# Float64 weights made float32 by a product on ScalarE instead of a clamp

## The chip, the core and the metric

The kernel runs on one core of one Trainium2 chip. The core has a matrix engine (TensorE; PE in the profile, and PEld for its weight loads), VectorE (DVE), ScalarE (ACT), GpSimd (POOL) and SyncE (SP), which here issues the loads. Each engine works through its own queue of instructions in order, and engines wait for each other by semaphores. The metric is the time of one execution on the device, in microseconds.

## What is computed

Three stages follow each other. Attention over 4 batches of 8 heads with 1152 positions of width 64, whose queries are pooled in pairs to 576; a mixing of the positions with two thin matrices and a two-layer network; and a gated unit with a normalisation and a product over positions:

```python
q_pool = q.reshape(B, H, S // 2, 2, D).mean(axis=3)
attn = softmax(scale * q_pool @ k.T) @ v           # 4 x 8 x 576 x 64
x = attn laid out as B x 576 x 512
u = x + ((x.T @ U) @ V).T                          # U 576 x 32, V 32 x 576
x = u + relu(u @ w_ch1) @ w_ch2                    # 512 x 2048, 2048 x 512
h = relu(x @ w_in); u, v = halves of h             # 512 x 1024
v_s = w_spatial @ normalised(v) + b_spatial
out = (u * v_s) @ w_out                            # 512 x 512
```

U, V, w_ch1, w_ch2, w_in and w_out are drawn as float32 and multiplied by a float64 number, so that they reach the kernel as float64. The core reads such a weight as two words of 32 bits, a low and a high one, and has to make a float32 of them.

## The kernel before

**Stages.** The attention is cut into units of 128 pooled queries (one head, or two halves of two heads); a unit is a set of score matmuls over 1152 keys, a row maximum, an exponential and the product with the values. The first five pairs of heads (units 0 to 44) take an extra step for the row's maximum ("peak"): a small product whose result, a row of 1x128, ScalarE copies out of PSUM into the tile of the queries' low part, and the next score matmuls read that tile. Beside the units of the attention the mixing and the network of each batch run as soon as its heads are there, and behind them comes the gated unit.

**Weights.** The weights are converted while the attention runs. Generators prepare w_ch2 and w_ch1 in two halves h (`w2_prep`, `w1_prep`); they are advanced between unit 13 and unit 39 for h = 0 and between unit 39 and unit 59 for h = 1. `low_rank_weights` converts U and V at the start. `w_in_split` and `w_split` convert w_in and w_out much later, at 748 to 896 us of the profiled execution. The first half of w_ch1 comes in four chunks of 128x1024 values, each loaded by SyncE into a buffer (tiles 113, 114 and 115 of the group ml), converted into tile 110, squared back into its buffer for a norm, and split into two 16-bit halves scaled by that norm. The buffers of the first half are three and are used in turn, also by w_ch2, so the load of a chunk has to wait until ScalarE has written the last square into its buffer. The first and the fourth chunk of w_ch1 use tile 113.

**The conversion.** `conv64_part` makes float32 from the words in five steps: Abs of the high word on ScalarE, taken as a float32; a clamp of that value between two constants; a shift by three with a mask on VectorE; the sign and top bit from the high word, by a mask and an or; and the low word's upper bits, by a shift and an or. The clamp holds the exponent where the shift can't overflow. It is 36 times an instruction of GpSimd (for U, V, w_ch1 and w_ch2) and 24 times one of VectorE (for w_in and w_out).

**What sets the order.** The kernel's functions issue nothing by themselves. A recorder takes each operation with what it reads and writes, gives it a cost by engine and size (`charge`, lines 174 to 210; a clamp on GpSimd counts 250 ns and 0.85 ns for each column and holds a port that VectorE's larger operations need as well), and a list scheduler puts all of them in an order, forwards by a priority and backwards by the latest start, eight times over, and takes the order that ends first (`issue`, lines 293 to 316). It does so three times in the program. Every instruction is issued from line 316, so the profile shows line 316 for all of them, and operations are told apart by engine and tile: `at` is attention, `ml` weights and the network, `co` small statistics, `ma` the gated unit, `xa` its weights, `ps` PSUM.

## Time and profile before

| | us |
|---|---|
| median of three runs | 1043.31 |
| lowest and highest run | 1041.41, 1043.6 |
| span of the profiled execution | 1043.4 |
| TensorE busy in it | 983.6 |
| VectorE busy | 778.7 |
| ScalarE busy | 631.8 |
| GpSimd busy | 310.6 |

The profiled execution is one run of the program, seen by the profiler; its span goes from the first to the last instruction. Its time stands 0.1 over the median. A number in brackets at the end of a row of the timeline is the idle time of the engine just before that row, and the arrow names what ended it. The granted clock is TensorE's; 1.00 is 2.4 GHz and 0.50 is 1.2 GHz.

### The profile page before, as it was taken

Reading aid. Unit: us, or ns where it says so; the run is one execution under the profiler, and the core shown is the slowest. Engines: PE = TensorE matmul, PEld = TensorE weight load, DVE = VectorE, ACT = ScalarE, POOL = GpSimd, SP = SyncE. Lnnn points to the kernel's source line nnn. Section 1 sums busy time; section 2 is a strip of 40 time slices with the busy share of each in tenths; the row PEclk is TensorE's granted clock in tenths of the full one; section 3 lists DMA queues with packets and bytes.
Section 4 is the critical chain, followed back from the end, with each engine's and each line's share of the span. In section 5 each row is a group of like instructions: output and inputs, shape, how many; then the busy total and the mean of one; then the engine's idle time right before and its main releaser. Section 6 shows DMA issues by size and latency. Waiting matters only on the chain.

```text
span 1043.4 us, 26123 instructions
## 1 busy us (share of the span) xinstructions
PE 983.6 (94%) x10797; PEld 790.5 (76%) x10797; DVE 778.7 (75%) x1645; ACT 631.8 (61%) x1170; POOL 310.6 (30%) x342
## 2 busy tenths in 40 slices
PE   4888889989899999999999999999899999999998
PEld 3677778768777778778887878888677857784787
DVE  5796879899998889888788998755693289646540
ACT  6776797877785667667666766654471147344322
POOL 1544445155442433345342533331000005002100
PEclk9998999999999999999999999999999999999999
DMA  9964446289988979899796988676460062220002
GB/s 240 241 166 107 115 109 153 73 190 210 175 162 140 195 130 198 157 156 183 137 200 102 192 165 124 117 136 116 159 203 1 30 213 86 68 71 29 3 1 92
DMA packets 270616, 139.34 MB, mean 134 GB/s; under 512 B 249152, under 2 KB 254016, under 8 KB 269472
## 3 DMA queue, kind: packets, MB, share of 16 engines
q1 hardware_dynamic: 270496, 137.67, 61.8%
q8 instruction: 84, 1.38, 0.5%
q14 instruction: 36, 0.29, 0.1%
HBM read 69.29 MB, written 9.44 MB: 75 GB/s over the span
## 4 chain that ended last, share of the span: by engine, by line
PE 63%; DVE 15%; DMA 8%; ACT 7%; issue 4%; POOL 2%; SPq 1%; ACTq 0%; DVEq 0%; POOLq 0%
PE ps L316 63%; DVE co L316 7%; ACT at L316 4%; DVE at L316 3%; DVE ml L316 3%; DMA ml<-in_w_dram 3%; DMA at<-at 3%; ACT ml L316 3%; POOL at L316 1%; SPq L316 1%; DMA at<-in_kT_dram 1%; DVE xa L316 1%; DVE ma L316 1%; DMA at<-in_qT_dram 1%; DMA at<-in_v_dram 1%
## 5 line engine op out<-in xcount | busy, mean ns | idle before, releaser
L316 PE MATMUL ps<-ml,ml 128*128 128x288 f16 x3072 | 410.5, 287 | 9.6 <-DVE ml L316 5.1
L316 PEld LDWEIGHTS <-ml 128*128 128x128 f16 x3072 | 290.6, 98 | 95.3 <-issue 24.2
L316 PE MATMUL ps<-at,at 128*64 128x65 f32 (+6 forms) x2892 | 246.3, 279 | 24.9 <-ACT at L316 24.4
L316 PEld LDWEIGHTS ps<-at,at 128*64 128x64 f32 (+2 forms) x2892 | 197.4, 162 | 54.0 <-ACT at L316 34.9
L316 DVE TENSOR_REDUCE co<-ps 128x1 f32<-128x1152 f32 (+1 forms) x166 | 200.6, 1210 | 48.2 <-PE ps L316 33.7
L316 ACT ACTIVATE at<-ps,co 128x1152 f32<-128x1152 f32 x99 | 120.7, 1219 | 64.4 <-DVE co L316 60.3
L316 POOL TENSOR_TENSOR at<-at 128x1152 f16<-128x1152 f32 (+1 forms) x54 | 114.8, 2127 | 62.0 <-ACT at L316 29.9
L316 ACT ACTIVATE ml<-ps 128x288 f16<-128x288 f32 x128 | 51.8, 406 | 89.1 <-PE ps L316 89.0
L316 PE MATMUL ps<-ma,ma 128*128 128x288 f16 (+2 forms) x676 | 105.2, 318 | 0.0
L316 POOL TENSOR_SCALAR co<-co,co 128x1 f32<-128x1 f32 x99 | 39.7, 401 | 217.9 <-ACT at L316 206.1
L316 PEld LDWEIGHTS <-at 128*128 128x128 f16 (+1 forms) x2970 | 90.6, 101 | 13.6 <-issue 7.4
L316 ACT CAST at<-at 128x1152 f16<-128x1152 f32 (+3 forms) x90 | 93.1, 1044 | 11.0 <-PE ps L316 5.5
L316 PE MATMUL ps<-at 128*128 128x64 f16 (+1 forms) x2970 | 95.3, 194 | 3.2 <-DVE co L316 2.2
L316 PE MATMUL ps<-xa,xa 128*128 128x288 f16 (+1 forms) x600 | 94.8, 320 | 1.3 <-ACT ma L316 1.3
L316 PEld LDWEIGHTS <-xa 128*128 128x128 f16 x600 | 58.5, 98 | 36.7 <-issue 2.0
L316 POOL TENSOR_TENSOR at<-at,at 128x1152 f16<-128x1152 f32 (+2 forms) x30 | 68.7, 2290 | 43.9 <-ACT at L316 41.7
L316 DVE SCALAR_TENSOR_TENSOR ml<-ps,ml 128x288 f16<-128x288 f32 x128 | 57.6, 451 | 31.1 <-ACT ml L316 30.5
L316 ACT ACTIVATE at<-at 128x1152 f16<-128x1152 f32 (+1 forms) x61 | 65.7, 1076 | 13.5 <-PE ps L316 9.4
L316 ACT ACTIVATE at<-ps 128x512 f32<-128x512 f32 (+2 forms) x100 | 57.7, 602 | 19.7 <-PE ps L316 18.9
L316 DVE SCALAR_TENSOR_TENSOR ml<-ml,co,ml 128x288 f16<-128x288 f32 (+1 forms) x85 | 63.4, 771 | 3.4 <-ACT ml L316 3.4
L316 ACT ACTIVATE ml<-ml,co 128x288 f16<-128x288 f32 (+2 forms) x96 | 52.1, 592 | 10.8 <-DVE co L316 9.7
L316 ACT CAST ma<-ma 128x288 fp32r<-128x288 f32 (+1 forms) x50 | 24.8, 498 | 53.6 <-DVE ma L316 53.5
(85 smaller groups left out, 1114.8 us busy)
## 6 DMA issues: line engine op xcount, KB each, us to landing
at<-in_qT_dram SPq DMA_DIRECT2D x42, 288.0 KB, 5.0
at<-in_kT_dram SPq DMA_DIRECT2D x42, 288.0 KB, 4.8
xa<-x2d SPq DMA_DIRECT2D x16, 576.0 KB, 4.9
ml<-in_w_dram SPq DMA_DIRECT2D x8, 1024.0 KB, 6.1
at<-in_v_dram SPq DMA_DIRECT2D x11, 576.0 KB, 4.9
ml<-in_w_dram SPq DMA_DIRECT2D x8, 512.0 KB, 6.7
at<-in_w_dram SPq DMA_DIRECT2D x8, 512.0 KB, 4.3
xa<-in_w_in_dram SPq DMA_DIRECT2D x8, 512.0 KB, 4.9
```

The lines of the kernel that those rows point to most:

```text
L316: getattr(eng, method)(*args, **kwargs)
```

## The change

The clamp goes. ScalarE multiplies the high word, taken as a float32, with 2 to the -112, which moves the exponent to its place and makes a number that is too small a zero; the shift's mask then keeps the whole exponent, and the sign alone comes from the high word. The two switches that chose the clamp's engine go as well.

```diff
-CL = 0
-CL1 = 0
...
-TOPBITS = -0x40000000
-F64MIN = 2.0 ** -15 * 1.125
-F64MAX = 122879.9921875
+SIGNBIT = -0x80000000
+F64SC = 2.0 ** -112
...
-    def conv64_part(F, raw, clamp):
+            conv64_part(F[:, i * n:(i + 1) * n], raw[:, i * n:(i + 1) * n, :])
+
+    def conv64_part(F, raw):
         lo, hi = raw[:, :, 0], raw[:, :, 1]
         Fi = F.bitcast(I32)
-        act.activation(F, hi.bitcast(F32), AF.Abs)
-        clamp = clamp or (dve if CL else pool)
-        clamp.tensor_scalar(F, F, F64MAX, F64MIN, op0=ALU.min, op1=ALU.max)
-        dve.tensor_scalar(Fi, Fi, 3, 0x3FFFFFF8, op0=ALU.logical_shift_left, op1=ALU.bitwise_and)
-        dve.scalar_tensor_tensor(Fi, hi, TOPBITS, Fi, op0=ALU.bitwise_and, op1=ALU.bitwise_or)
+        act.activation(F, hi.bitcast(F32), AF.Copy, scale=F64SC)
+        dve.tensor_scalar(Fi, Fi, 3, 0x7FFFFFF8, op0=ALU.logical_shift_left, op1=ALU.bitwise_and)
+        dve.scalar_tensor_tensor(Fi, hi, SIGNBIT, Fi, op0=ALU.bitwise_and, op1=ALU.bitwise_or)
         dve.scalar_tensor_tensor(Fi, lo, 29, Fi, op0=ALU.logical_shift_right, op1=ALU.bitwise_or)
...
-                conv64_part(Fs[i + k], words(a, DM), dve if CL else pool)
+                conv64_part(Fs[i + k], words(a, DM))
...
-            conv64(F, words(t, n), dve if CL1 else pool)
+            conv64(F, words(t, n))
...
-        conv64(F, words(t, n), dve)
+        conv64(F, words(t, n))
...
-            conv64(Fs[i], words(t, DM), dve)
+            conv64(Fs[i], words(t, DM))
```

The instruction counts of the two programs differ by 36 on GpSimd (tensor-scalar operations, 135 before and 99 after) and by 24 on VectorE (483 and 459). Each program has two loads of ScalarE's function tables. The scheduler solves the order anew: the matmuls stand in another order up to the one with the number 6698 of 9790 and alike from there on, which is at about 745 us of the profiled execution. The instructions now carry line 313.

The first place is ScalarE's queue at the first chunk of w_ch1 (first half). `ml_113,co_131` is the Square out of the chunk's buffer for an earlier part of w_ch2, `ml_110<-ml_113` the chunk's conversion; `at_104<-ps_70` are exponentials, `at_100` and `at_101` the tiles that the peaks are copied to. Before, from the first row behind the last Square `ml_113,co_131`:

```order
L316 ACTIVATE at_104<-ps_70 128x320
L316 CAST at_98<-at_97 128x576
L316 CAST at_93<-at_92 128x1152
L316 ACTIVATE at_104<-ps_70 128x512
L316 CAST at_100<-at_97 64x576
L316 ACTIVATE ml_115,co_142<-ml_110 128x512
L316 ACTIVATE at_104<-ps_70 128x512
L316 CAST at_101<-ps_70 1x128
L316 ACTIVATE ml_115,co_142<-ml_110 128x512
L316 ACTIVATE at_104<-ps_70 128x256
L316 ACTIVATE at_104<-ps_70 128x512 x2
L316 ACTIVATE ml_110<-ml_113 128x512 x2
```

After, from the fourth row behind the last Square `ml_113,co_131`:

```order
L313 ACTIVATE at_104<-ps_70 128x640
L313 ACTIVATE ml_115,co_142<-ml_110 128x512
L313 ACTIVATE at_104<-ps_70 128x640 x2
L313 CAST at_101<-ps_70 1x128
L313 ACTIVATE ml_108<-ml_110,co_150 128x512
L313 ACTIVATE at_104<-ps_70 128x640
L313 CAST at_98<-at_97 128x576
L313 CAST at_93<-at_92 128x1152
L313 CAST at_101<-ps_70 1x128
L313 ACTIVATE at_104<-ps_70 128x320
L313 CAST at_100<-at_97 64x576
L313 ACTIVATE ml_110<-ml_113 128x512
```

Before, the last Square out of the buffer has eleven rows between it and the conversion; after, it stands four rows ahead of this piece, with fourteen rows between it and the first conversion, and the chunk's two halves are converted apart from each other.

The second place is ScalarE's queue at the fourth chunk, which uses the same buffer. `ml_113,co_141` are the Squares of the first chunk, `ml_110<-ml_113` again the conversion. Before, from the second Square:

```order
L316 ACTIVATE ml_113,co_141<-ml_110 128x512
L316 CAST at_100<-ps_70 1x128
L316 ACTIVATE ml_110<-ml_110,co_149 128x512
L316 ACTIVATE ml_108<-ml_110,co_149 128x512
L316 CAST ml_108<-ml_110 128x512
L316 ACTIVATE at_104<-ps_70 128x512
L316 ACTIVATE at_104<-ps_70 128x256
L316 ACTIVATE at_104<-ps_70 128x512
L316 CAST at_100<-ps_70 1x128
L316 ACTIVATE at_104<-ps_70 128x512
L316 ACTIVATE ml_110<-ml_114 128x512 x2
L316 CAST at_100<-ps_70 1x64
```

After, from the two Squares:

```order
L313 ACTIVATE ml_113,co_141<-ml_110 128x512 x2
L313 ACTIVATE at_104<-ps_70 128x320
L313 CAST at_99<-at_97 128x576
L313 CAST at_94<-at_91 128x1152
L313 CAST at_100<-ps_70 1x128
L313 CAST at_101<-at_97 64x576
L313 ACTIVATE ml_110<-ml_110,co_149 128x512
L313 ACTIVATE ml_108<-ml_110,co_149 128x512
L313 CAST ml_108<-ml_110 128x512
L313 ACTIVATE ml_110<-ml_113 128x512
L313 ACTIVATE ml_110<-ml_114 128x512
L313 CAST at_100<-ps_70 1x128
```

Before, the conversion of the fourth chunk comes as the second row behind this piece, behind another small cast, thirteen instructions after the second Square. After, it is the tenth row of the piece, eight instructions after the second Square, and the third chunk's conversion (`ml_110<-ml_114`) and a peaks' copy come behind it.

## Rows read from the trace of the kernel before

**Rows 1.** The page's busy time, share of the span and instructions of each engine.
```profile
PE 983.6 (94%) x10797; PEld 790.5 (76%) x10797; DVE 778.7 (75%) x1645; ACT 631.8 (61%) x1170; POOL 310.6 (30%) x342
```

**Rows 2.** Windows by stage: length, engines' busy us, granted clock, DMA share, GB/s.
```profile
14.00:330.00 316.00, 281.96 (x3643) 239.55 (x3643) 270.38 (x490) 236.91 (x464) 138.23 (x144) 0.98 0.71 160
330.00:740.00 410.00, 403.20 (x5096) 329.06 (x5093) 325.76 (x620) 260.05 (x429) 144.45 (x165) 1.00 0.83 150
...
748.00:839.00 91.00, 91.00 (x745) 72.70 (x744) 54.68 (x171) 39.81 (x91) 0.00 (x0) 1.00 0.24 81
839.00:876.00 37.00, 35.43 (x206) 19.94 (x205) 31.95 (x94) 22.75 (x49) 10.45 (x9) 1.00 0.63 199
```

**Rows 3.** Waits of TensorE, 0 to 330 us: total us, times, longest.
```profile
PE ps L316 <- ACT at L316: 24.5, 19, 9.8
PE ps L316 <- DVE co L316: 14.9, 15, 1.9
```

**Rows 4.** Timeline around the longest wait: start, us, instruction, idle before and its releaser.
```profile
85.70 1.21 ACT L316 ACTIVATE ml<-ml 128x512 f32<-128x512 f32 x2 [3.66 <-DMA ml<-in_w_dram]
...
86.94 0.26 ACT L316 CAST at<-ps 1x128 fp32r<-1x128 f32 x1
...
87.24 4.83 PE L316 MATMUL ps<-at,at 128*128 128x384 f32 x45 [4.40 <-ACT at L316]
```

**Rows 5.** Chain of waits, 70 to 112 us: issue, us to landing, transfer.
```profile
75.42 10.20 DMA ml<-in_w_dram
...
100.84 8.07 DMA ml<-in_w_dram
```

**Rows 6.** Windows around the longest wait and around one at 43.67 us.
```profile
40.00:60.00 20.00, 17.64 (x251) 15.03 (x250) 15.55 (x19) 16.88 (x34) 12.56 (x13) 1.00 0.73 201
...
87.20:91.80 4.60, 4.56 (x43) 4.23 (x45) 3.60 (x5) 2.74 (x4) 1.85 (x2) 0.50 0.02 8
```

**Rows 7.** Timeline of TensorE at 43.67 us.
```profile
43.67 1.64 PE L316 MATMUL ps<-at,at 128*128 128x384 f32 x37 [1.62 <-ACT at L316]
```

**Rows 8.** Groups by line and form, ScalarE: busy us, mean ns, idle before.
```profile
L316 ACT ACTIVATE at<-at 128x1152 f16<-128x1152 f32 x50 | 58.1, 1163 | 2.0 <-DMA at<-at 1.2
L316 ACT CAST at<-at 128x1152 f16<-128x1152 f32 x49 | 56.4, 1151 | 0.7
```

**Rows 9.** Groups by line and form, weights (ml) and late weights (xa).
```profile
L316 POOL TENSOR_SCALAR ml<-ml 128x512 f32<-128x512 f32 x32 | 22.7, 714 | 40.5 <-ACT ml L316 39.9
...
L316 DVE TENSOR_SCALAR ml<-ml 128x512 int32<-128x512 int32 x32 | 17.5, 563 | 5.9 <-POOL ml L316 5.9
...
L316 DVE TENSOR_SCALAR xa<-xa 128x256 f32<-128x256 f32 x24 | 6.3, 282 | 0.0
```

**Rows 10.** Waits of VectorE, whole span: total us, times, longest.
```profile
DVE ml L316 <- POOL ml L316: 7.3, 6, 3.9
```

**Rows 11.** Timeline of GpSimd and VectorE behind the longest wait.
```profile
86.44 1.19 POOL L316 TENSOR_SCALAR ml<-ml 128x512 f32<-128x512 f32 x2 [5.47 <-ACT ml L316]
...
87.09 0.82 DVE L316 TENSOR_SCALAR ml<-ml 128x512 int32<-128x512 int32 x1 [3.86 <-POOL ml L316]
```

**Rows 12.** Timeline of ScalarE, 69 to 79 us.
```profile
69.52 0.43 ACT L316 COPY ml<-ps 128x320 f32<-128x320 f32 x1
...
77.86 0.66 ACT L316 CAST at<-at 64x576 fp32r<-64x576 f32 x1
```

**Rows 13.** The page's DMA issues: KB each, median us to landing.
```profile
ml<-in_w_dram SPq DMA_DIRECT2D x8, 1024.0 KB, 6.1
```

**Rows 14.** Timeline of ScalarE, 96 to 110 us.
```profile
96.47 2.29 ACT L316 CAST at<-at 128x576 fp32r<-128x576 f32 x3
...
101.28 1.34 ACT L316 ACTIVATE ml<-ml,co 128x512 f32<-128x512 f32 x2 [1.14 <-DVE co L316]
...
108.94 1.23 ACT L316 ACTIVATE ml<-ml 128x512 f32<-128x512 f32 x2 [1.11 <-DMA ml<-in_w_dram]
```

**Rows 15.** View of the weight tiles: shortest, median, longest ns; first, last us.
```profile
L316 DVE TENSOR_SCALAR ml<-ml x36: 202/422/1853, 22.3 to 262.5; 128x512 int32<-128x512 int32 x32, 128x80 int32<-128x80 int32 x2, 96x288 int32<-96x288 int32 x2
```

More of the change, by code (lines that the diff above doesn't have):

```diff
@@ L498, in words, with conv64 @@
         return t[:, :2 * n].bitcast(I32).rearrange("p (n w) -> p n w", w=2)
-    def conv64(F, raw, clamp=None):
+    def conv64(F, raw):
         n = F.shape[1] // SPL
         for i in range(SPL):
-            conv64_part(F[:, i * n:(i + 1) * n], raw[:, i * n:(i + 1) * n, :], clamp)
-    def conv64_part(F, raw, clamp):
+            conv64_part(F[:, i * n:(i + 1) * n], raw[:, i * n:(i + 1) * n, :])
+    def conv64_part(F, raw):
         lo, hi = raw[:, :, 0], raw[:, :, 1]
         Fi = F.bitcast(I32)
-        act.activation(F, hi.bitcast(F32), AF.Abs)
-        clamp = clamp or (dve if CL else pool)
-        clamp.tensor_scalar(F, F, F64MAX, F64MIN, op0=ALU.min, op1=ALU.max)
-        dve.tensor_scalar(Fi, Fi, 3, 0x3FFFFFF8, op0=ALU.logical_shift_left, op1=ALU.bitwise_and)
-        dve.scalar_tensor_tensor(Fi, hi, TOPBITS, Fi, op0=ALU.bitwise_and, op1=ALU.bitwise_or)
+        act.activation(F, hi.bitcast(F32), AF.Copy, scale=F64SC)
+        dve.tensor_scalar(Fi, Fi, 3, 0x7FFFFFF8, op0=ALU.logical_shift_left, op1=ALU.bitwise_and)
+        dve.scalar_tensor_tensor(Fi, hi, SIGNBIT, Fi, op0=ALU.bitwise_and, op1=ALU.bitwise_or)
         dve.scalar_tensor_tensor(Fi, lo, 29, Fi, op0=ALU.logical_shift_right, op1=ALU.bitwise_or)
```

## The prediction

> **What bounds the kernel now.** I read first the engines' shares, then the busy time by stage, then TensorE's waits, and last the instructions around its longest wait. The shares say that TensorE is the engine to look at: it is busy for 983.6 of 1043.4 us, every other engine for at most 778.7 [rows 1]. So the whole program has about 60 us in which TensorE does nothing, and a change that leaves the matmuls alone can win or lose only there, or by moving the granted clock.
>
> The windows by stage say where these 60 us lie [rows 2]. From 14 to 330 us, the stretch in which the weights U, V, w1 and w2 are converted beside the first attention pairs, TensorE is idle for 316.00 - 281.96 = 34.0 us. From 330 to 740 it is idle for 6.8 us of 410. From 748 to 839, where w_in is converted, it is busy for 91.00 of 91.00 us. From 839 to 876, where most of w_out is converted, 1.6 us are left. So what happens on ScalarE, VectorE or GpSimd before 330 us can matter, what happens from 748 to 839 is covered, and a delay or a gain before 330 us is neither absorbed nor doubled later: with 6.8 us of idle time in the next 410 us there is almost no slack in which to hide it.
>
> Inside the first 330 us TensorE waits mostly for ScalarE's attention tiles, 24.5 us in 19 waits (the longest of 9.8 us is the start of the program), and for VectorE's small statistics, 14.9 us in 15 waits [rows 3]. One of these waits touches the conversion. At 87.24 us TensorE has been idle for 4.40 us and is released by ScalarE. ScalarE's own row explains it: at 85.70 it starts the Abs of the first chunk of w1 after 3.66 us of waiting for the transfer of that chunk, and the copy of the peaks, 0.26 us of work that the score matmuls need, stands behind it and starts at 86.94 [rows 4]. The transfer was issued at 75.42, when ScalarE had finished the last Square out of that buffer, and took 10.20 us [rows 5]. The stall has a second price: in the 4.60 us behind it the granted clock is 0.50, that is 1.2 instead of 2.4 GHz, with TensorE busy for 4.56 us [rows 6]. At the full clock this is 2.28 us of work, so 2.28 us are lost. The stall costs 4.40 + 2.28 = 6.7 us in all. A wait need not drop the clock: the one of 1.62 us at 43.67 lies in a window whose clock is 1.00 [rows 6, 7].
>
> **The change part by part.** The sum is made against the profiled execution, whose span is 1043.4 us, 0.1 over the median of 1043.31 us. Four edits are in the diff, and a fifth effect comes from the list scheduler, which solves the order anew once the clamps are gone.
>
> *The operation on ScalarE.* Abs of the high word becomes a copy with a constant scale, the same shape, the same count of 60 (36 for the early weights, 24 for w_in and w_out). The trace has a scaled copy and a plain one of the same shape 128x1152, 1163 and 1151 ns [rows 8]. The constant scale thus costs about 12 ns, 60 x 12 ns = 0.7 us if all of it lay on the path, with nothing as the lower end. I take 0.
>
> *The clamps of w_in and w_out, on VectorE.* 24 instructions of 282 ns are 6.8 us by the mean and 6.3 us by the group's busy time, which counts overlap once [rows 9]. Those of w_in lie where TensorE is busy all the time, and what covers them is the last w1/w2 block's matmuls. Only from 839 to 876 can they show, where TensorE is idle for 1.6 us [rows 2]. Bounds: 0 to -1.6 us; I take -0.5, because most of that idle time belongs to one wait for the gated unit's tiles, not for weights.
>
> *The clamps of the early weights, on GpSimd.* The 32 large ones take 714 ns each, 22.7 us [rows 9], and four small ones add little. GpSimd is busy for 310.6 of 1043.4 us [rows 1] and is no bound; what the clamp costs is a step in the chain ScalarE, GpSimd, VectorE. VectorE waits for GpSimd's weight tiles 7.3 us in 6 waits, the longest 3.9 us [rows 10]. That longest one is the stall above seen from VectorE, which starts the shift at 87.09 [rows 11], so it is counted already. 7.3 - 3.9 = 3.4 us is the most that VectorE gets back; TensorE waits for VectorE only at times, so I take -1.0, between 0 and -3.4.
>
> *The new order at the first chunk of w1.* In the order after, the two Squares out of the buffer stand early, and between the second of them and the conversion there are 15 ScalarE instructions, among them five exponentials and three long casts. In the trace of before nearly the same rows run from the copy at 69.52 to the end of the cast at 77.86, which is 78.52: 9.0 us [rows 12]. After has one Square less and one scaled copy and two tiny casts more, so I estimate 9 us again. The transfer is issued at the start of this stretch instead of its end. It needs 6.1 us (the median of these eight transfers, [rows 13]) to 10.20 us [rows 5]. The head of line then waits 0 to 1.2 us; I take 1.0, nearer to the slow row because it is the same transfer, and no loss of clock, as at 43.67. Gain: 1.0 - 6.7 = -5.7 us, bounds -6.7 and -5.5.
>
> *The new order at the fourth chunk of w1.* It uses the same buffer, and here the order goes the other way. Before, the transfer was issued at 100.84, took 8.07 us, and ScalarE waited 1.11 us for it at 108.94 [rows 5, 14]; thirteen instructions lay in between. After, both Squares stand together and only eight instructions follow before the conversion. Their durations: an exponential of 320 columns, 0.43 (a copy of this size, [rows 12]); the casts of 576, 1152 and 576 columns, 2.29 together [rows 14]; the peaks' copy, 0.26 [rows 4]; two scaled halves, 1.34 [rows 14]; one cast of 512, half of 1.21 = 0.60 [rows 4]. The sum is 4.9 us. With a transfer of 6.1 to 8.07 us ScalarE waits 1.2 to 3.2 us instead of 1.11, and the peaks' copy that TensorE needs stands two rows behind. I take 2.1, net +1.0 us. Bounds: -1.1, if a wait of ScalarE for VectorE in that stretch covers it, and +6.4, if the transfer is as slow as the first chunk's and the clock falls (the slower rival, below).
>
> *The rest of the new order.* Apart from the stall TensorE has 34.0 - 4.4 = 29.6 us of idle time before 330 us, made of some forty short waits. They will be dealt out anew, and the trace of before doesn't show the outcome. Bounds: -2, two waits of about a microsecond less (14.9/15, [rows 3]), and +6, a new stall nearly as dear as the one that goes. I take +2, the middle: the end of one wait lets the next one show.
>
> The sum: 0 - 0.5 - 1.0 - 5.7 + 1.0 + 2.0 = -4.2 us, 1043.4 - 4.2 = **1039 us**.
>
> A rule on the port that VectorE and GpSimd share asks for a larger gain. The row first: at 86.44 GpSimd runs two clamps, 1.19 us long, until 87.63. VectorE starts a shift at 87.09 that takes 0.82 us and ends at 87.91, though the median of the 36 shifts is 0.42; the longest took 1.85 and the 32 large ones have a mean of 563 ns [rows 9, 11, 15]. The Trainium skill, "SBUF — State Buffer", section "SBUF: two separate sides", states that this port pair is an exclusive lock, so that a VectorE operation in its two-port mode and a GpSimd operation block each other for a whole instruction. The row agrees in direction. By that rule 36 GpSimd operations fewer would also shorten VectorE's own instructions, and the sum would be that of the first rival; the forecast leaves them as they are.
>
> **The rivals.**
>
> *The lock goes as well.* VectorE's shifts fall from their mean to their median: 32 x (563 - 422) ns = 4.5 us [rows 9, 15]; GpSimd's step of the chain is worth its whole bound of 3.4; the first and fourth chunks and w_out count as in the forecast, -5.7 + 1.0 - 0.5; and the rest of the order costs nothing. The sum is -13.1 us, 1030 us. For it: VectorE is busy for 270.38 of 316 us before 330 us [rows 2] and TensorE waits for it. Against it: a shorter instruction of VectorE shows only in those of its waits that TensorE shares, 14.9 us in all [rows 3], and the removed clamps may be followed by GpSimd's other work in the same place.
>
> *The gain is given back.* The stall at 87 us goes, but TensorE meets other waits before 330 us for as much: the rest of the order costs its upper bound of 6 instead of 2. Sum -0.2, 1043.2 us: no change that can be measured. For it: 29.6 us of short waits show that ScalarE and VectorE run just abreast of TensorE there, and ScalarE's in-order queue has the same rows as before. Against it: the stall is by far the longest wait after the start.
>
> *The fourth chunk's transfer becomes the stall (slower).* If that transfer takes 10.20 us, as the first chunk's did, ScalarE waits 10.20 - 4.9 = 5.3 us in front of a peaks' copy. At 87 us a wait of 3.66 left TensorE idle for 4.40, 0.7 more [rows 4], so it idles for 6.0, the clock's 2.3 come on top, and the first chunk keeps its wait of 1.2. 6.0 + 2.3 + 1.2 = 9.5 stands against 6.7 + 1.1 before: +1.7. The clamps gain nothing then, since VectorE and GpSimd wait for the same transfer; the rest of the order costs its 2. The sum is +3.7, 1047 us. It decides where the transfer exceeds some 8.5 us. For it: 8.07 and 10.20 us are both rows of this buffer, and DMA engines were 0.71 busy in this stage [rows 2]. Against it: the median is 6.1.
>
> *The change doesn't do what it says.* The scaled copy of words could be dearer than Abs, or need the function table loaded anew. Both orders have two table loads, and the nearest rows bound the product at 0.7 us, inside every range above, so it gets no chance of its own.
>
> **How the numbers follow.** The forecast, 1035 to 1041 us, gets 0.45; the lock, 1028 to 1035, gets 0.10; the gain given back, 1041.3 to 1045.4, gets 0.20; slower, above 1045.4, gets 0.25. 0.2%, about what a measurement of this kernel can tell from no change, is 2.1 us, so the first two are faster (0.55), the third the same (0.20), the last slower (0.25). The range is 1032 to 1048 us: below it lies half of the lock's chance, above it the tail of the slower case, 0.12 or so together; all terms at one end at once (1029 and 1051) are left out.
>
> **What would show it.** After should have no GpSimd group of 32 tensor-scalar weights; TensorE busy for 983 to 984 us again; no wait of TensorE over 2 us between 14 and 330 us, and a clock of 1.00 from 80 to 100 us; its idle time in that stage near 30 instead of 34.0 us; ScalarE's wait for the transfer in front of the first chunk's conversion at or under 1.6 us and in front of the fourth's at 1.2 to 3.2 us; VectorE's wait for GpSimd's weight tiles gone; windows behind 748 us alike within 2 us. If TensorE's idle time there stays at 34 with other waits, the gain was given back; if the mean of VectorE's shift falls to 0.42 us, the lock's part is right. The prediction is wrong if a transfer behind another queue's work, which the order doesn't show, holds ScalarE or TensorE at a new place for over 4 us, or if the stage from 330 us on no longer follows TensorE's matmuls alone.

## The result

The changed kernel is slower. It takes 1048.66 us (median of 13 runs, 1045.27 to 1053.34) against 1043.08 us for the kernel before (13 runs, 1038.54 to 1048.69). The two medians alone give 1.0053; the ratio on record for the two sets of runs is 1.0065, with an interval from 1.0046 to 1.0084. A second set of runs, with its own runs of before beside it, gave 1.0050 (1.0025 to 1.0075). The forecast was 1039 us and faster.

One thing has to be known before any two profiles are compared here: the time of one and the same kernel moves by some 10 us from run to run, and a profile is one execution. The profiled execution of after has a span of 1045.7 us and was timed at 1047.45 us, so 1.7 us lie around the span. The 14 profiled executions of this study for which both numbers exist differ by 1.7 to 2.2 us. With that, the profiled execution of before (span 1043.4) belongs to a time of some 1045 us (an estimate from these margins), 2 us above the median of its kernel, while after's lies 1.2 us below its own. The two profiles are only 2.3 us apart; the medians are 5.6 us apart.

### The profile page after: what moved, and what is told of

It is laid out like the page before. It is cut to its first block, busy times and chain, and to the rows that moved or that the text cites. A ratio compares the mean times of both kernels' runs of the same rounds, so it can differ in the third digit from the quotient of the medians.

```text
span 1045.7 us, 26074 instructions
## 1 busy us (share of the span) xinstructions
PE 986.8 (94%) x10797; PEld 789.4 (75%) x10797; DVE 766.9 (73%) x1621; ACT 631.3 (60%) x1170; POOL 283.8 (27%) x306
## 4 chain that ended last, share of the span: by engine, by line
PE 67%; DVE 11%; ACT 8%; DMA 7%; issue 4%; SPq 1%; POOL 1%; ACTq 0%; DVEq 0%; POOLq 0%
PE ps L313 67%; DVE co L313 5%; ACT at L313 4%; DMA at<-at 4%; DVE ml L313 4%; DVE at L313 2%; ACT ml L313 2%; SPq L313 1%; ACT ma L313 1%; DMA at<-in_kT_dram 1%; POOL at L313 1%; DMA ml<-in_w_dram 1%; DMA at<-in_w_dram 1%; DVE xa L313 1%; DMA at<-in_v_dram 0%
## 5 line engine op out<-in xcount | busy, mean ns | idle before, releaser
L313 PEld LDWEIGHTS ps<-at,at 128*64 128x64 f32 (+2 forms) x2892 | 195.3, 160 | 53.4 <-ACT at L313 33.8
L313 ACT CAST at<-at 128x1152 f16<-128x1152 f32 (+3 forms) x90 | 92.8, 1045 | 16.8 <-PE ps L313 7.1
L313 POOL TENSOR_TENSOR at<-at,at 128x1152 f16<-128x1152 f32 (+2 forms) x30 | 66.5, 2216 | 65.0 <-ACT at L313 62.8
L313 DVE SCALAR_TENSOR_TENSOR ml<-ml,co,ml 128x288 f16<-128x288 f32 (+1 forms) x85 | 66.0, 805 | 1.2 <-ACT ml L313 0.8
```

The source lines that it names most:

```text
L313: getattr(eng, method)(*args, **kwargs)
```

## The profile after

The page of after, its engines (answers to [rows 1]):

```profile
PE 986.8 (94%) x10797; PEld 789.4 (75%) x10797; DVE 766.9 (73%) x1621; ACT 631.3 (60%) x1170; POOL 283.8 (27%) x306
```

GpSimd does 26.8 us less and VectorE 11.8 us less, ScalarE the same. TensorE, the engine that sets the time, is busy for 3.2 us more with the same 10797 matmuls. The windows by stage (answer to [rows 2]; length, busy time of TensorE, its weight loads, VectorE, ScalarE, GpSimd, then granted clock, DMA share, GB/s):

```profile
14.00:330.00 316.00, 284.27 (x3649) 238.72 (x3649) 271.59 (x492) 238.22 (x465) 109.51 (x108) 0.98 0.70 159
330.00:740.00 410.00, 402.81 (x5090) 328.04 (x5088) 316.80 (x617) 258.17 (x428) 146.75 (x166) 1.00 0.82 150
...
748.00:839.00 91.00, 91.00 (x738) 72.36 (x736) 50.52 (x153) 40.18 (x92) 0.00 (x0) 0.99 0.24 80
839.00:876.00 37.00, 36.45 (x214) 20.77 (x212) 31.32 (x92) 22.05 (x48) 9.50 (x9) 1.00 0.61 198
```

From 14 to 330 us GpSimd's 28.7 us are gone, and TensorE's idle time fell from 34.0 to 31.7 us. But its busy time grew by the same 2.3 us, for six matmuls more, so the stage won nothing. From 839 to 876 us TensorE is busier because its wait now falls behind 876. The groups of the conversion (answers to [rows 8] and [rows 9]; busy us, mean ns, idle before):

```profile
L313 ACT ACTIVATE at<-at 128x1152 f16<-128x1152 f32 x50 | 58.1, 1162 | 2.7 <-DMA at<-at 2.1
...
L313 ACT ACTIVATE ml<-ml 128x512 f32<-128x512 f32 x48 | 30.9, 651 | 8.0 <-DVE ml L313 5.0 <-DMA ml<-in_w_dram 2.5
...
L313 DVE TENSOR_SCALAR ml<-ml 128x512 int32<-128x512 int32 x32 | 17.4, 549 | 3.5 <-ACT ml L313 3.3
```

The scaled copy takes what Abs took: the group of 48 operations of that form which holds the 32 large conversions has a mean of 651 ns in both profiles. Its row before:

```profile
L316 ACT ACTIVATE ml<-ml 128x512 f32<-128x512 f32 x48 | 30.6, 651 | 8.0 <-DMA ml<-in_w_dram 5.9 <-DVE ml L316 1.6
```

VectorE's shift takes 549 ns instead of 563.

The stall that the forecast built on is gone. The timeline of after at the first chunk of w_ch1 (start, length, instruction, idle before; answers to [rows 4]):

```profile
75.21 0.26 ACT L313 CAST at<-ps 1x128 fp32r<-1x128 f32 x1
...
76.39 0.69 ACT L313 ACTIVATE ml<-ml 128x512 f32<-128x512 f32 x1
```

```profile
75.52 2.11 PE L313 MATMUL ps<-at,at 128*128 128x384 f32 x41 [0.64 <-ACT at L313]
```

The conversion starts at 76.39 and waits for no transfer, and TensorE waits 0.64 us instead of 4.40. In exchange the clock falls elsewhere. Windows of after around three drops:

```profile
80.00:104.00 24.00, 20.19 (x297) 17.50 (x297) 20.13 (x36) 15.96 (x32) 8.64 (x6) 1.00 0.59 134
104.00:110.00 6.00, 6.00 (x33) 5.81 (x33) 4.92 (x10) 4.42 (x12) 0.29 (x2) 0.72 0.01 4
176.00:186.00 10.00, 7.37 (x35) 6.13 (x34) 7.15 (x13) 6.13 (x14) 0.29 (x2) 0.83 0.30 49
296.00:306.00 10.00, 6.58 (x53) 4.74 (x52) 9.58 (x15) 8.34 (x13) 4.72 (x8) 0.83 1.10 211
```

Busy time times what is missing from a clock of 1.00 is what a drop costs: 6.00 x 0.28 = 1.7 us, 7.37 x 0.17 = 1.3 and 6.58 x 0.17 = 1.1 in these windows. The two wide ones mix idle time into the clock; windows of 2 us give 1.7, 1.7 and 1.3. Each drop follows idle time of TensorE; the first one follows 2.53 us at 103.51, the longest wait of after behind the start:

```profile
103.51 0.49 PE L313 MATMUL ps<-co,co 128*128 128x128 f32 x2 [2.53 <-DVE co L313]
```

Behind the attention, at 877.90, TensorE waits longer for ScalarE's copies out of PSUM than before (2.19 instead of 1.31 us); first the row of after, then that of before:

```profile
877.90 1.63 PE L313 MATMUL ps<-xa,xa 128*128 128x288 f16 x12 [2.19 <-ACT ma L313]
```

```profile
875.61 1.63 PE L316 MATMUL ps<-xa,xa 128*128 128x288 f16 x12 [1.31 <-ACT ma L316]
```

**How the runs below are compared.** All kernels pass one point at which the order of TensorE is the same: the long row of matmuls of the network's last batch, right behind the attention (744.20 us in before, 744.26 in after). Its start tells what the first part took; the rest of the span tells the second. The lost clock is the sum over all windows of 2 us up to that point of busy time times the missing share of the clock, the idle time the sum of what TensorE was not busy in them. The late wait is TensorE's in the two rows above. The ratios and intervals are those on record for 6 to 13 runs of a kernel against runs of before beside them. They are not quotients of the two medians (earlyonly has 1.0032 on record and 1.0048 by the medians, peakfirst 0.9965 and 0.9975), so differences of some 0.1% between rows tell nothing. The other columns come from one profiled execution each.

| kernel | ratio to before | interval | first part, us | of it idle | lost clock | rest of span | late wait |
|---|---|---|---|---|---|---|---|
| before | 1 | | 744.20 | 55.1 | 4.0 | 299.2 | 1.31 |
| planonly | 0.9993 | 0.9965 to 1.0021 | 744.26 | 55.6 | 4.7 | 299.8 | 1.16 |
| lateonly | 1.0030 | 1.0009 to 1.0051 | 739.67 | 52.6 | 2.4 | 302.0 | 2.20 |
| squareslater | 1.0009 | 0.9991 to 1.0027 | 738.66 | 52.5 | 1.8 | 301.2 | 2.29 |
| after | 1.0065 | 1.0046 to 1.0084 | 744.26 | 53.4 | 5.0 | 301.4 | 2.19 |
| afteragain | 1.0050 | 1.0025 to 1.0075 | 743.72 | 52.5 | 6.5 | 302.6 | 2.19 |
| earlyonly | 1.0032 | 1.0010 to 1.0054 | 744.16 | 53.4 | 5.0 | 299.9 | 1.31 |
| reducefirst | 1.0063 | 1.0038 to 1.0088 | 746.26 | 53.7 | 6.3 | 301.9 | 2.19 |
| clampback | 1.0213 | 1.0182 to 1.0244 | 757.99 | 65.0 | 4.8 | 307.4 | 2.86 |
| redrawa | 1.0060 | 1.0037 to 1.0083 | 750.51 | 59.0 | 5.1 | 301.8 | 2.19 |
| redrawb | 1.0026 | 1.0002 to 1.0049 | 747.68 | 54.0 | 9.8 | 299.6 | 0.76 |
| oldredrawa | 1.0073 | 1.0047 to 1.0099 | 749.38 | 55.6 | 3.9 | 299.3 | 1.48 |
| oldredrawb | 1.0013 | 0.9992 to 1.0034 | 749.02 | 54.6 | 10.1 | 299.8 | 1.37 |
| oldpeakfirst | 0.9982 | 0.9963 to 1.0000 | 742.99 | 55.1 | 3.5 | 300.5 | 1.32 |
| peakfirst | 0.9965 | 0.9944 to 0.9986 | 739.43 | 53.1 | 1.9 | 300.2 | 1.16 |

## The experiments

### The arithmetic alone, the order alone

My theory after the result was that the new order costs, not the arithmetic. Its rival was that the product on ScalarE, or the missing clamp as such, is what is slow. Two kernels cross the two.

`planonly`: after's arithmetic, but the clamp is still given to the scheduler and only not issued (two lines more than after's `conv64_part`; the arguments that hand the clamp's engine down are left out here).

```diff
         act.activation(F, hi.bitcast(F32), AF.Copy, scale=F64SC)
+        clamp.tensor_scalar(F, F, F64MAX, F64MIN, op0=ALU.min, op1=ALU.max)
+        rec.ops[-1].calls.clear()
```

> After's arithmetic in before's order: the clamp is still given to the scheduler with its engine and cost, but no instruction is issued for it. If the new order is what costs (my theory now), the time is that of before or a little under it, 1040 to 1043 us, since work goes and no order changes. If the product on ScalarE or the missing clamp itself costs, it is that of after, about 1048 us.

Measured: 0.9993 (0.9965 to 1.0021). In before's order the new arithmetic is neither dearer nor measurably cheaper: 60 instructions of GpSimd and VectorE fewer bring nothing that can be measured. The interval reaches from 3.7 us less to 2.2 us more, so after's 1.0046 and above lies outside it, and the 1.5 us that the forecast gave the clamps lies inside.

`clampback`: before's arithmetic in after's order; the clamp is issued ahead of the shift that needs it, without a place in the plan (the one line that does it; the lines that let an operation call another engine are left out).

```diff
+        rec.ops[-1].calls.insert(0, (clamp.name + ".tensor_scalar", (F, F, F64MAX, F64MIN), dict(op0=ALU.min, op1=ALU.max)))
```

> Before's arithmetic in after's order: the scheduler plans without the clamps, and each clamp is issued on its old engine right ahead of the shift that needs it. If the new order costs, 1048 us or up to 4 us more, since the clamps are work that no one planned for. If the arithmetic costs, about 1043 us.

Measured: 1.0213, some 16 us more than after, far over what was expected. VectorE's waits (total us, times, longest) and the clamp's group show where:

```profile
DVE ml L315 <- POOL ml L315: 20.5, 17, 3.0
```

```profile
L315 POOL TENSOR_SCALAR ml<-ml 128x512 f32<-128x512 f32 x32 | 22.7, 713 | 16.4 <-ACT ml L315 16.0
```

The same 22.7 us of clamps that cost nothing measurable in an order planned for them cost over ten (the first part alone is 13.7 us longer than after's) in one that isn't: VectorE waits 20.5 us for them instead of 7.3 [rows 10]. So removal of work is not the term that decides here, but how well the order fits the work.

### Which half of the change

`lateonly` takes the clamp from w_in and w_out alone, `earlyonly` from the early weights alone. In the first, the order up to 745 us is before's, in the second after's. The lines are those of `lateonly` against after, at one early and one late weight: `pool` stands for the clamp on GpSimd, `None` for the product. In `earlyonly` the early weights have `None` and the late ones `dve`, the clamp on VectorE.

```diff
-            conv64(F, words(t, n))
+            conv64(F, words(t, n), pool)
...
-            conv64(Fs[i], words(t, DM))
+            conv64(Fs[i], words(t, DM), None)
```

> The clamp goes from w_in and w_out alone (24 instructions of VectorE); the order up to 745 us is that of before. If the order of the first part costs, 1042 to 1043.5 us. If the loss lies behind 745 us, where the profiles differ by 2.3 us (1.4 of the clock, 0.9 of a wait for ScalarE at 877 us), 1045 us or more.

> The clamp goes from U, V, w_ch1 and w_ch2 alone (36 instructions of GpSimd); the order up to 745 us is that of after, and w_in and w_out keep their clamps. If the order of the first part costs, about 1048 us. If the loss lies behind 745 us, about 1043 us.

Measured: 1.0030 and 1.0032. Neither theory had it alone; both halves lose about 3 us by the ratios (2.9 and 5.1 by the medians, 1045.35 and 1047.55 against 1042.5), and together they make after's 1.0050 to 1.0065. The profiles of the two parts agree in direction with both. Behind the common point ScalarE, VectorE and TensorE of `lateonly` stand as in after, and those of `earlyonly` as in before. The rest of the span is 301.2 to 302.6 us in the five profiles with after's late order (after, afteragain, lateonly, squareslater, reducefirst) and 299.2 to 300.5 us in the five with before's (before, planonly, earlyonly, oldpeakfirst, peakfirst). The first part is 738.7 to 744.3 us in the four unaltered executions of before's order and 743.7 to 744.3 in the three of after's.

`lateonly` also showed, without being meant to, why the forecast's largest term was wrong. Its order is before's to the instruction, and ScalarE's timeline agrees with before's within hundredths of a us from 75 to 82 us. Here is the place of the stall in `lateonly`, ScalarE and then TensorE, and its windows:

```profile
81.92 1.23 ACT L316 ACTIVATE ml<-ml 128x512 f32<-128x512 f32 x2
83.17 0.26 ACT L316 CAST at<-ps 1x128 fp32r<-1x128 f32 x1
```

```profile
83.48 2.82 PE L316 MATMUL ps<-at,at 128*128 128x384 f32 x45 [0.63 <-ACT at L316]
```

```profile
80.00:92.00 12.00, 11.37 (x174) 10.17 (x176) 11.35 (x21) 10.07 (x21) 4.59 (x5) 1.00 0.40 84
```

No wait for the transfer, no stall, no drop of the clock: the same 45 matmuls take 2.82 instead of 4.83 us. The transfer that took 10.20 us in before's profile was there in time here, though the load was issued at the same point of the program. In the four executions of before's order it was late twice (before, planonly) and in time twice (lateonly, squareslater), and the first part took 744.2 and 744.3 us with the stall and 739.7 and 738.7 without. The two kernels with a swap further down load the chunk at the same place: it was late in `oldpeakfirst` (10.11 us) and in time in `peakfirst`. The times of `planonly` look like two cases as well: six of its 12 runs took 1036.8 to 1040.7 us, the other six 1044.9 to 1048.4, and the profiled one, which has the stall, is of the second group.

The traces' single DMA packets narrow the late transfer down. The chunk's 1 MB goes in 128 packets of 8192 bytes, whose median time is 0.31 us. In before all but eight had ended at 79.68 us. One of the eight, begun at 78.37, took 2.11 us, and seven more ran behind it, each starting within 0.1 us of the end of the one before, till 85.15. `planonly` (1.97 us from 79.00, then seven more till 85.69) and `oldpeakfirst` (1.22 us from 77.79, then seven more till 83.86) show the same; in the three executions in time the last packet ended at 80.26, 82.17 and 81.31. So the load as a whole is not slower in the late executions: one string of eight packets is. Eight is also what each of the core's 16 DMA engines gets of 128 packets if they are dealt out evenly (an estimate; the traces don't say which engine took a packet). What holds that string isn't shown.

### Is after's order a bad one, or before's a lucky one?

The scheduler was asked for other orders by counting 1 ns more for each ScalarE operation (a), or 2 ns more for each VectorE operation (b), with after's arithmetic (`redrawa`, `redrawb`) and with before's (`oldredrawa`, `oldredrawb`).

```diff
-            op.cost += (51 if psum else 93) + 93 * ptr + n * 0.833
+            op.cost += (52 if psum else 94) + 93 * ptr + n * 0.833
```

```diff
-            op.cost += 75 + (55 if ptr else 0) + n * (0.52 if fast else 1.04)
+            op.cost += 77 + (55 if ptr else 0) + n * (0.52 if fast else 1.04)
```

> After with its order drawn anew: the scheduler counts 1 ns more for each ScalarE operation, nothing else changes. If the missing clamp makes the orders worse (it paced VectorE), 1046 us or more again. If after's order is one draw out of many, it may land anywhere from 1038 to 1052.

> After with its order drawn anew in another way: 2 ns more for each VectorE operation. The same two theories: 1046 or more if it is systematic, anywhere from 1038 to 1052 if it is a draw.

> Before with its order drawn anew: 1 ns more for each ScalarE operation. If before's order is a lucky draw, it gets slower, 1045 us or more, with the same arithmetic. If orders with the clamp are good as such, 1041 to 1044.

> Before with its order drawn anew in the second way: 2 ns more for each VectorE operation. If before's order is a lucky draw, 1045 us or more, like the first redraw with the clamps (1051) and the two without (1047 and 1051). If the first redraw was the unlucky one, 1041 to 1044.

Measured: 1.0060 and 1.0026 without the clamps, 1.0073 and 1.0013 with them. All four are slower by the median than the order that the kernel before had, three of them by more than their interval, and the pair with the clamps spans as much as the pair without. One or two nanoseconds of planned cost, which change no instruction, move the kernel by as much as the change did. So after's order is an ordinary draw, and before's is a better one than these four neighbours. That the missing clamps make orders worse as a rule isn't borne out: the means, 1.0043 and 1.0043, are the same. Two draws of each kind don't tell how wide the spread is.

### Single waits

`reducefirst` takes the longest early wait of after: on VectorE, one row maximum goes ahead of four conversion steps of the third chunk.

```diff
+TENSOR_REDUCE co_119<-ps_70 128x1
 TENSOR_SCALAR ml_110<-ml_110 128x512
 SCALAR_TENSOR_TENSOR ml_110<-ml_114,ml_110 128x512 x3
-TENSOR_REDUCE co_119<-ps_70 128x1
```

> After, with one row maximum moved on VectorE ahead of four conversion steps of the third chunk of w_ch1 (a shift and three ors, 3.2 us in the profile). In after's profile TensorE idles for 2.53 us at 103.5 behind that row maximum, and the clock loses 1.7 us behind it. If this is where the first part of the new order loses, the wait falls under 1 us and the median by 2.5 to 4 us, to 1.002 to 1.004 of before. If the idle time only moves to the next wait, it stays at 1.006 to 1.007.

> The changed kernel once more, beside the run above on the same chip, and a second profile of it. If the first result holds, 1.005 to 1.008 of before, and the same three drops of the clock near 104, 180 and 300 us as in its first profile. If the drops are chance, they stand elsewhere.

Measured: 1.0063 beside 1.0050 for after itself, so nothing won. The timeline of TensorE in `reducefirst`:

```profile
102.25 0.49 PE L315 MATMUL ps<-co,co 128*128 128x128 f32 x2 [1.52 <-DVE co L315]
102.49 0.59 PE L315 MATMUL ps<-at,at 128*128 128x384 f32 x2
104.82 1.44 PE L315 MATMUL ps<-co,at 96*128 96x256 f32 x5 [1.74 <-DVE at L315]
```

The wait of 2.53 us became 1.52, since the row maximum now waits for TensorE itself, and a new one of 1.74 us came 2 us later: the tile that TensorE wants next (`at`, 32x128) now stands behind the same conversion steps. The idle time only moved. The second profile of after has the first and the third drop of the clock again (102 to 108 and 296 to 306 us), but not the one at 180; a new one stands at 222 to 226. Its lost clock up to the common point is 6.5 us. In the two executions of before's order without the stall it is 1.8 and 2.4.

`squareslater` took on the wait behind 850 us. In after's late order three Squares of the second norm stand on ScalarE ahead of the copy out of PSUM that releases TensorE. Two of them go behind it, in `lateonly`:

```diff
-ACTIVATE xa_10429,co_174<-xa_10429 128x1152
 ACTIVATE ma_11506<-ps_70,co_177 128x288
...
-ACTIVATE xa_10430,co_174<-xa_10430 128x1152
...
 ACTIVATE ma_11513<-ps_70,co_177 128x512
+ACTIVATE xa_10429,co_174<-xa_10429 128x1152
+ACTIVATE xa_10430,co_174<-xa_10430 128x1152
```

> The kernel without the late clamps alone (1.003), with two Squares of the second norm (128x1152, 1.4 us each with their accumulators) moved on ScalarE behind the last copy out of PSUM of the first normalisation. If they make TensorE's wait of 2.2 us at 872 us, that wait falls to 0.8 to 1.3 us, since another tile of the group is ready only 1.4 us earlier, and the median falls by 1 to 2.5 us to 1042 to 1044. If the wait is made by VectorE or GpSimd, it stays at 2.2.

The wait stayed, at 2.29 us, so moving the Squares away doesn't shorten it; the ratios (1.0009 against 1.0030, with intervals that overlap) don't tell the two kernels apart. The timeline of `squareslater` names what took over:

```profile
868.74 1.16 POOL L318 TENSOR_TENSOR ma<-ma,ma 128x512 f16<-128x512 f32 x1 [3.13 <-ACT ma L318]
868.75 1.89 DVE L318 TENSOR_SCALAR ma<-ma,co,co 128x512 f32<-128x512 f32 x2
...
870.21 0.62 ACT L318 CAST ma<-ma 128x512 f16<-128x512 f32 x1 [1.13 <-DVE ma L318]
...
871.45 0.68 ACT L318 ACTIVATE ma<-ps,co 128x512 f32<-128x512 f32 x1
```

ScalarE now comes earlier to its cast, GpSimd starts its subtraction earlier, and that subtraction runs at the same moment as VectorE's two normalisations, which take 1.89 us together. In `lateonly`, where GpSimd was idle at that moment, the same two take 1.00:

```profile
869.51 1.00 DVE L316 TENSOR_SCALAR ma<-ma,co,co 128x512 f32<-128x512 f32 x2
```

ScalarE waits the 1.13 us for them in its queue, and the copy that frees TensorE starts at 871.45 instead of 871.56. What makes the wait 0.9 us longer than in before's late order is thus open: it is the order, but no single instruction of it that I moved.

The wait has a second price. The row of TensorE behind it in `lateonly`:

```profile
872.30 2.84 PE L316 MATMUL ps<-xa,xa 128*128 128x288 f16 x12 [2.20 <-ACT ma L316]
```

The 12 matmuls take 2.84 us, where they take 1.63 in before and after, since the clock has fallen (0.66 from 871 to 876 us). It falls there in `lateonly`, `afteragain` and `reducefirst`, three of the five profiles with after's late order, and in none of the five with before's.

### The version that beats both

The stall of before's order needs no new plan. One swap on ScalarE, made when the instructions are issued, puts the peaks' copy ahead of the first chunk's conversion. `peakfirst` does it in `planonly`, `oldpeakfirst` in before, clamps and all.

```diff
+CAST at_101<-ps_70 1x128
 ACTIVATE ml_110<-ml_113 128x512 x2
-CAST at_101<-ps_70 1x128
```

> After's arithmetic in before's order, with one swap: the peaks' copy that stood behind the conversion of the first chunk of w_ch1 goes ahead of it on ScalarE. In one profile of this order the transfer of that chunk took 10.4 us and TensorE idled for 4.6 us, in another there was no such wait and the matmul that follows the attention came 4.6 us earlier. If the slow transfer is in about half of the executions, the median falls by about 3 us against before, to 1039 to 1040, and the slowest runs (1045 to 1049) get rarer. If the stall is no price of the median, it stays at 1042 to 1043.

> Before, clamps and all, with the one swap on ScalarE: the peaks' copy goes ahead of the conversion of the first chunk of w_ch1. If the swap alone made the gain of the product with the swap (0.9965), this is as fast, 1039 to 1041 us. If the missing clamps had a part in it, it stays nearer to before, 1042 us or more.

Measured: 0.9965 (0.9944 to 0.9986) and 0.9982 (0.9963 to 1.0000). With the product the swap makes a kernel that is faster than before and, set against after's 1.0050 and 1.0065, 0.9 to 1.0% faster than after. By the medians it is 1041.33 against 1043.98 us, and before with the swap 1043.11 against 1043.87, a time that the expectation gave to the case in which the missing clamps have a part. But the intervals of the two overlap, and `planonly`'s overlaps with both, so neither that part nor the swap's own is shown. The slowest of 12 runs took 1045.1 and 1045.3 us, against 1049.3 and 1049.2 for the 29 runs of before beside each. The profile of `oldpeakfirst` is of an execution with a late transfer, and shows what the swap does there; ScalarE, TensorE and the window:

```profile
81.70 0.26 ACT L318 CAST at<-ps 1x128 fp32r<-1x128 f32 x1 [0.49 <-PE ps L318]
84.78 1.21 ACT L318 ACTIVATE ml<-ml 128x512 f32<-128x512 f32 x2 [2.82 <-DMA ml<-in_w_dram]
```

```profile
88.31 0.49 PE L318 MATMUL ps<-co,co 128*128 128x128 f32 x2 [3.48 <-DVE co L318]
```

```profile
82.00:94.00 12.00, 8.52 (x128) 7.75 (x129) 8.07 (x12) 7.70 (x15) 3.06 (x4) 1.00 0.18 40
```

The peaks' copy is out at 81.70 and TensorE runs its 47 matmuls, but then it waits 3.48 us for the next row maximum, since VectorE, too, works in order and waits with its shift for the late chunk:

```profile
86.17 0.82 DVE L318 TENSOR_SCALAR ml<-ml 128x512 int32<-128x512 int32 x1 [3.78 <-POOL ml L318]
86.92 1.34 DVE L318 TENSOR_REDUCE co<-ps 128x1 f32<-128x1152 f32 x1
```

So in such an execution the swap saves 0.9 us of idle time and the drop of the clock, which is 1.00 in this window: about 3.2 us, with the 2.28 us that the prediction read for the drop. If half of the executions are late, as three of these six were, that is some 1.6 us on average (an estimate). The 0.9982 of `oldpeakfirst` fits it; `peakfirst` gains more, and what the rest is isn't shown. The shift stands ahead of the row maximum on VectorE just as the conversion stood ahead of the copy on ScalarE; moving that as well wasn't tried.

## Why the prediction was wrong, step by step

In the sum of the forecast three terms failed: the first chunk's gain of 5.7 us counted a stall that half of the executions don't have, the rest of the order was set at 2 us and cost 4.1 to 5.6, and the late clamps were priced as work alone at -0.5, where their new order cost about 2.

**What bounds the kernel** held. TensorE's idle time and its clock decide, the time from 748 to 839 us is covered (91.00 of 91.00 us busy again), and the 410 us in the middle follow TensorE (7.2 us of idle time, 6.8 before).

**The operation on ScalarE, 0 taken**, held: 651 ns in both, and `planonly` at 0.9993.

**The clamps of GpSimd, -1.0 taken**, were worth nothing that can be measured. The 7.3 us of VectorE's waits for GpSimd [rows 10] are gone, and its waits for ScalarE's weight tiles grew in their place, from 33.9 to 40.5 us (43.2 in `planonly`, which keeps before's order). VectorE's waits for the tiles of the group `ml`, first in before, then in after:

```profile
DVE ml L316 <- ACT ml L316: 33.9, 44, 1.5
...
DVE ml L313 <- ACT ml L313: 40.5, 50, 1.8
DVE ml L313 <- PE ps L313: 32.1, 24, 2.4
```

**The late clamps, -0.5 taken**, had the wrong sign. I priced the work that goes and not the order that changes with it: `lateonly`, which has this edit alone, is 1.0030, and `squareslater`, with the same late order but for two moves, 1.0009 with an interval that holds 1. Some 2 us show in the profiles as a longer second part: 1.9 us between the means of the five profiles with either late order, of which 1.0 is idle time (4.6 against 3.6) and 0.9 lost clock (3.2 against 2.2). Most of the idle time is the wait for ScalarE, a wait I had found in the trace and put down as idle time that could only shrink.

**The first chunk, -5.7 taken**, is the step that failed worst, though the mechanism is right. The new order loads the chunk earlier (issued at 67.37, converted at 76.39, 9.0 us later as estimated), and its conversion waits for no transfer in any of the four profiles of this order without the clamps (after, afteragain, earlyonly, reducefirst). But the stall that goes was in two of four executions of before's order and not in the others; with it the first part took 4.5 to 5.6 us longer than without. The term should have been about half as large, and a profiled execution that stood some 2 us above the median of its kernel was taken for its middle. The comparison of span and median, "0.1 over", was made between two unlike numbers: 1.7 to 2.2 us lie around the span.

**The fourth chunk, +1.0 taken, and the slower rival** were wrong. The load was issued at 88.10, and ScalarE waited 0.61 us for it at 93.55, less than the 1.11 of before [rows 14], so that transfer was no stall. The chunk was there 5.45 us after the issue, sooner than the quickest transfer that the term used (6.1). The upper bound of this term was also added up short: it takes 5.3 us of idle time where the slower rival takes 6.0, with which it is +7.2 and not +6.4. No measured time turns on it.

```profile
93.55 0.68 ACT L313 ACTIVATE ml<-ml 128x512 f32<-128x512 f32 x1 [0.61 <-DMA ml<-in_w_dram]
```

**The rest of the order, +2 taken between -2 and +6**, carried the result. Against executions of before's order without the stall, the first part of after's order is 4.1 to 5.6 us longer in its three profiles: at most 0.9 us in idle time, 2.6 to 4.7 us in lost clock, and the rest, up to 1.5 us, in busy time that these sums don't explain. I had counted idle time as the price of a wait and charged the clock to one stall only; here the idle time stayed nearly the same and the clock lost most of the time. The prediction's own signs say so too: TensorE is busy for 986.8 us where it named 983 to 984, and waits 2.53 us once where it named no wait over 2. The four redraws say why a middle value with a gain in sight was the wrong guess: the order at hand was better than the four drawn beside it, which the profile of before could not show.

**The rivals.** "The gain is given back" was nearest, and fell short of what happened. "The lock goes as well" was wrong in its size: the mean of the shifts fell from 563 to 549 ns, not to 422, and the longest is 1.84 us after 1.85. The clamps had a part in it all the same. A large shift that runs beside no GpSimd operation takes 0.42 us on average in both profiles. In before 14 of the 32 run beside one for some time, in after still 8, and four of its five longest beside the attention's work, as the rival's own counterargument said; one of them:

```profile
98.55 1.43 POOL L313 TENSOR_TENSOR at<-at 128x576 f32<-128x576 f32 x1 [3.88 <-DMA at<-in_qT_dram]
...
98.94 1.31 DVE L313 TENSOR_SCALAR ml<-ml 128x512 int32<-128x512 int32 x1
```

In `planonly`, before's order without the clamps, the mean is 495 ns, so the missing clamps alone give back 68 of the 141 ns that the rival counted, and the new order takes most of that away. None of it is seen in the kernel's time.

**The sum that can be accounted for.** By the profiles, the first part costs 2.4 us (mean of after, afteragain and earlyonly 744.0, mean of the four executions of before's order 741.7) and the second about 2 us, 4 to 4.5 us together. The ratios say 5.2 to 6.8 us, the medians 3.4 and 5.6. The difference lies within what single executions move by. Still open: what holds eight packets of the first chunk's transfer in some executions and not in others, though nothing differs in how the program issues it; which instruction of the late order makes its wait; and what after's longest runs (six of 23 above 1050 us, none of them profiled) have that its two profiles don't.

## What to carry to other kernels

Where a scheduler places the instructions, an edit that removes work buys a new order with it, and the price of that order is a term of its own, centred above zero when the old order was the best of several. Keep the old order and make the edit in it (plan the removed instruction, don't issue it) to know what the edit itself is worth; then mend the order by hand at the wait that the trace names. And before a term is built on one stall, ask whether other executions have it: compare the profiled run's own time, span and margin together, with the spread of the runs.

## What the runs showed of the hardware

A load of 1 MB issued at the same place of the same order took over 10 us in three executions (10.20, 10.37 and 10.11) and left ScalarE with no wait of more than 0.31 us in three others. In the late ones eight of its 128 packets ran behind each other, some 5 us longer than all others. Between the profiles, one late load and the drop of the clock behind it account for about 5 us; the runs of one kernel spread over 10.

Clock drops of about 1.5 us each come behind several short waits as well as behind one long one: at 178 us of after TensorE met 0.54, 0.95 and 0.51 us within 3 us, and the window from 176 to 186 has a clock of 0.83.

VectorE's operations took longer beside a GpSimd operation: 1.89 against 1.00 us for the same pair of normalisations, and up to 1.85 against 0.42 us for a shift. The Trainium skill, "SBUF — State Buffer", section "SBUF: two separate sides", calls the port pair that the two engines share an exclusive lock; these operations agree with that in direction. The pair shows that it can undo a gain: what came earlier on ScalarE made VectorE's work fall beside GpSimd's.
